# Chunked attention and a multiplicative FFN: half of the partition moves on ScalarE's queue, with another written-out order

## The chip, the cores and the metric

The kernel runs on one core of one Trainium2 chip. The metric is the time of one execution on the device in microseconds; lower is better. The kernel before took 247.61 us (median of 3 runs, 247.45 to 247.93).

A core has five engines that run their own instruction streams side by side: PE (TensorE, matrix products into PSUM), DVE (VectorE), ACT (ScalarE), POOL (GpSimd) and SP (SyncE). In this kernel POOL only issues loads and SP only issues moves and stores. Semaphores order the engines among each other. [...]

## The reference, cut to what matters

```python
batch, n_heads, seq, head_dim = (8, 8, 576, 64)          # q, k, v
chunk = 64; nc = S // chunk; scale = 1.0 / np.sqrt(D)
scores = scale * np.matmul(q_c, k_c.transpose(0, 1, 2, 4, 3))   # 64 x 64 in each chunk and head
attn = softmax(scores)                                   # exp, divided by the row's sum
out = np.matmul(attn, v_c)
x = out.transpose(0, 2, 1, 3).reshape(B * S, H * D)      # 4608 tokens x 512
a = x @ w1; b = x @ w2                                   # 512 -> 1024
return ((a * b) @ w3) @ w_out                            # 1024 -> 1024 -> 512
```

So 4608 tokens go through an attention within chunks of 64 tokens, and then through a feed-forward part. The kernel computes w3 @ w_out once (w3o) and so needs one product less for each token.

## The kernel before, in words

Tokens are handled in 18 pieces p of 256 (four chunks); two pieces make a group g = p // 2 of 512 tokens. Every step of the work has a letter and numbers, and the string ORDER (line 9) lists all steps in program order. The last loop of the kernel (line 412) walks through that string and emits the instructions of each step. All instructions are marked to stay in program order on their engine, so the string is the schedule: it sets the order on each engine's queue and, with it, the order of loads, moves and stores. There is no planner at run time.

The steps of attention for piece p are:

- q, k, v: loads from HBM, cast to bf16, on POOL's queue (`load`, L95). For the first piece q and k come through R (on SP and ACT) and are cast by K on ACT.
- T p.s (L188, DVE): transposes q (s=0) or k (s=1) in blocks of 32 x 32 into qkT.
- G g.a (`do_G`, L192, p of 8 and more): four moves between partitions each, qkT to qkm, 128 KB a move, so that the scores need half as many products. Pieces below 8 go without.
- S (PE): the scores, 64 small products; E (ACT): their exponential; P (PE): times v, with a column of ones for the row's sum; N p.u (DVE): reciprocal and product for half a piece, into xn.
- X p.u (DVE): transposes xn into xt (p below 8) or into xm, from which H g.a (`do_H`, L276) moves the blocks into xt by four moves of 64 KB each.

The steps of the feed-forward part are A p.j and B p.j (PE: x @ w1 and x @ w2 for a part j of the 1024 columns; one pair fills one PSUM buffer), C (ACT, L317: copies a out of PSUM), M (DVE, L332: times b, into ab), O (PE: with w3o, 256 tokens), Y (ACT: copies O's result), Q (SP: stores 512 KB). For p below 4, A and B take one piece and two values of j's columns at once; from p = 4 on they take a whole group, so p is then even. The weights are loaded by i (w1 and w2, a quarter at a time), h (w3, half at a time) and o (w_out); V, W and Z make w3o. D is a number of products with zeros into a buffer that is used next; it has no effect on the result.

Each engine waits for what it reads and for the release of the buffer that it writes. Those that matter are: PSUM with four buffers shared by S, P (two each), A/B, W and O, given out in program order, so that each waits for the one given out four before it; qk with 5, vbuf with 6, qkT, qkm, xm, e and o_sb with 2, a_sb, ab and xn with 3, w3T and xt with 4.

All moves and stores of before go through one function, on SP's queue:

```python
def move(dst, src):
    inorder(nc.sync.dma_start(dst, src))          # L180
```

Of the kernel before, what the change touches and what calls it, by code (L numbers as in the profile page):

```python
# [7 lines left out]

ORDER = """
R0 R1 v0 q1 k1 v1 i0 i2 i1 q2 k2 i3 v2 q3 k3 v3 q4 k4 h0 o h1 v4 D0.0.0.16.64 K0 T0.0 K1 T0.1 q5 k5  # L10
v5 D0.0.0.8.512 S0 T1.0 E0 T1.1 q6 k6 P0 v6 S1 N0.0 E1 N0.1 X0.0 X0.1 A0.0 B0.0 C0.0 P1 M0.0 A0.2
N1.0 B0.2 N1.1 A0.1 X1.0 X1.1 C0.1 B0.1 C0.2 A1.0 T2.0 B1.0 C1.0 A1.1 M0.1 M0.2 B1.1 C1.1 T2.1 q7 k7
v7 A0.3 M1.1 S2 C0.3 M1.0 B0.3 E2 M0.3 P2 A1.2 T3.0 B1.2 N2.0 A1.3 N2.1 B1.3 C1.3 X2.0 C1.2 X2.1
T3.1 q8 k8 v8 A2.0 M1.2 C2.0 S3 T4.0 B2.0 E3 A2.1 M1.3 B2.1 M2.0 C2.1 T4.1 q9 k9 P3 v9 A2.2 M2.1
B2.2 N3.0 A2.3 X3.0 N3.1 S4 C2.3 C2.2 X3.1 B2.3 E4 M2.2 A3.3 M2.3 B3.3 V0 A3.2 V1 B3.2 C3.2 V2 C3.3
A3.1 W0 V3 M3.3 M3.2 A3.0 V4 B3.1 C3.0 V5 Z0 B3.0 W1 C3.1 M3.1 T5.0 W2 V6 Z1 V7 T5.1 q10 k10 W3 Z2
M3.0 T6.0 T6.1 S5 Z3 P4 v10 q11 k11 E5 O0 N4.0 T7.0 T7.1 N4.1 O1 Y0 X4.0 Q0 T8.0 T8.1 P5 v11 q12 k12
Y1 X4.1 O2 N5.0 Q1 T9.0 N5.1 S6 T9.1 O3 E6 X5.0 G4.0 Y2 X5.1 G4.1 P6 v12 q13 k13 A4.0 Y3 N6.0 B4.0
X6.0 C4.0 Q2 A4.1 N6.1 B4.1 M4.0 C4.1 X6.1 S7 M4.1 A4.2 E7 T10.0 B4.2 C4.2 T10.1 P7 v13 q14 k14 A4.3
M4.2 N7.0 B4.3 C4.3 A4.4 M4.3 A4.5 N7.1 C4.4 B4.4 X7.0 C4.5 S8 M4.4 S9 E8 B4.5 T11.0 A4.6 E9 M4.5  # L20
B4.6 C4.6 X7.1 P8 v14 q15 k15 M4.6 A4.7 T11.1 B4.7 C4.7 N8.0 A6.0 G5.0 B6.0 M4.7 C6.0 N8.1 A6.1 M6.0
B6.1 G5.1 C6.1 X8.0 A6.4 M6.1 P9 v15 q16 k16 C6.4 B6.4 N9.0 A6.2 M6.4 B6.2 X8.1 C6.2 N9.1 A6.5 X9.0
B6.5 M6.2 H4.0 A6.3 X9.1 B6.3 C6.3 C6.5 A6.6 M6.3 H4.1 B6.6 M6.5 C6.6 T12.0 A6.7 S10 M6.6 S11 Q3 E10
B6.7 T12.1 O4 E11 T13.0 C6.7 M6.7 T13.1 P10 v16 q17 k17 Y4 A8.3 G6.0 N10.0 B8.3 N10.1 C8.3 A8.0 M8.3
G6.1 B8.0 T14.0 C8.0 P11 v17 A8.2 M8.0 X10.0 B8.2 C8.2 N11.0 O5 X10.1 N11.1 M8.2 X11.0 A8.1 X11.1
H5.0 Y5 T14.1 A8.5 C8.1 A8.4 T15.0 B8.5 H5.1 C8.4 C8.5 B8.1 A8.6 M8.1 B8.4 M8.5 C8.6 S12 M8.4 S13
E12 B8.6 T15.1 A8.7 E13 M8.6 G7.0 B8.7 C8.7 P12 M8.7 A10.3 N12.0 B10.3 Q4 C10.3 G7.1 A10.0 M10.3
A10.1 N12.1 C10.0 B10.0 C10.1 Q5 P13 M10.0 B10.1 N13.0 A10.6 M10.1 B10.6 C10.6 N13.1 A10.2 X12.0 S14
M10.6 C10.2 S15 B10.2 E14 T16.0 O6 E15 M10.2 T16.1 T17.0 A10.5 T17.1 Y6 P14 B10.5 C10.5 G8.0 O7
M10.5 N14.0 N14.1 Q6 G8.1 X12.1 X13.0 P15 Y7 A10.4 N15.0 B10.4 Q7 N15.1 C10.4 O8 X13.1 M10.4 X14.0  # L30
X14.1 S16 Y8 S17 A10.7 E16 Q8 B10.7 H6.0 C10.7 O9 E17 M10.7 X15.0 H6.1 O10 Y9 Q9 H7.0 P16 Y10 A12.2
N16.0 B12.2 X15.1 C12.2 O11 N16.1 H7.1 M12.2 Q10 P17 Y11 A12.7 N17.0 B12.7 X16.0 C12.7 A12.3 N17.1
A14.5 M12.7 C12.3 A12.0 B12.3 A12.4 M12.3 B12.4 X16.1 C12.4 X17.0 C12.0 A12.6 C14.5 M12.4 H8.0 B14.5
C12.6 B12.0 M14.5 B12.6 M12.0 Q11 A12.5 X17.1 M12.6 B12.5 H8.1 A14.7 A14.6 C14.7 C12.5 B14.6 C14.6
M12.5 B14.7 M14.6 A14.1 M14.7 A14.3 A16.1 C14.3 B14.1 C16.1 C14.1 B16.1 M14.1 B14.3 A16.3 M14.3
B16.3 C16.3 A12.1 M16.3 A14.0 M16.1 B12.1 C14.0 C12.1 A16.6 M12.1 A14.4 B14.0 C14.4 A16.5 M14.0
B14.4 C16.6 B16.6 O12 M16.6 B16.5 Y12 O13 C16.5 Q12 M16.5 M14.4 A14.2 Y13 A16.2 C14.2 Q13 B16.2
C16.2 B14.2 A16.7 M14.2 A16.4 C16.7 B16.4 B16.7 O14 M16.7 M16.2 A16.0 B16.0 C16.0 C16.4 O15 Y14
M16.4 M16.0 Q14 O16 Y15 Q15 Y16 Q16 O17
"""  # L40


# [1 line left out]
def kernel(  # L44
# [11 lines left out]
    nc = tc.nc  # L56
# [30 lines left out]
    def inorder(ins):  # L87
        tc.keep_in_program_order(ins)
        return ins
# [83 lines left out]
    blk = [slice(i * BL, (i + 1) * BL) for i in range(NB)]  # L173
    qkT_t, qkm_t, s_t, e_t, pv_t, xn_t, xm_t, xt_t = {}, {}, {}, {}, {}, {}, {}, {}
# [1 line left out]

    def move(dst, src):
        inorder(nc.sync.dma_start(dst, src))  # L180

    def do_T(p, s, h=None):

# [8 lines left out]
    def do_G(g, a):  # L192

        if a == 0:
            qkm_t[g] = asb.tile([P, 2, 2, 2, H, CH], bf, tag="qkm", bufs=2, name="qkm")

        for i in (0, 2, 1, 3):
            e = (i + a) % 2
            move(qkm_t[g][blk[i // 2 * 2 + e], i % 2], qkT_t[g][blk[i], e])

    def do_S(p, hh=None):
        g, m = divmod(p, 2)
# [50 lines left out]
    def new_xt(g):  # L253

        if g not in xt_t:
            xt_t[g] = asb.tile([P, KO * GT], bf, tag="xt", bufs=4, name="xt")
        return xt_t[g]
# [18 lines left out]
    def do_H(g, a):  # L276

        xt = new_xt(g)[:].rearrange("p (s c) -> p s c", s=2)
        for i in (0, 2, 1, 3):
            move(xt[blk[i // 2 * 2 + a], i % 2], xm_t[g][blk[i], a].rearrange("p o m t -> p (o m t)"))  # L280

    ab_t, ps_t, a_t, o_t = {}, {}, {}, {}

# [50 lines left out]
    def store(p, u0, u1, n0, n1, o_sb):  # L334
        move(out[p * PT + u0 * UT:p * PT + u1 * UT, n0:n1].rearrange("(u p) n -> p u n", p=UT), o_sb)
# [63 lines left out]
    def load_half3(i):  # L399
# [7 lines left out]


    do = {"q": load_q, "k": load_k, "v": load_v, "i": load_w12, "o": load_wo, "h": load_half3, "T": do_T, "S": do_S, "R": do_R, "K": do_K, "E": do_E, "G": do_G, "H": do_H,
          "P": do_P, "N": do_N, "X": do_X, "A": do_A, "B": do_B, "C": do_C, "M": do_M, "D": do_D, "V": do_V,  # L410
          "W": do_W, "Z": do_Z, "O": do_O, "Y": do_Y, "Q": do_Q}
# [32 lines left out]
```

The softmax here doesn't subtract the row's maximum and nothing guards it: scores larger than these inputs give would overflow.

## Time and profile before

| what | before |
|---|---|
| median of 3 runs | 247.61 us |
| the profiled execution | 247.45 us |
| its span | 245.3 us |
| PE busy | 228.4 us |
| DVE busy | 152.4 us |
| ACT busy | 83.3 us |
| POOL busy | 82.9 us |
| bytes in DMA packets | 37.63 MB |

The span runs from the first instruction to the last one of the profiled execution. What its time has beyond the span lies around it. Busy time is the sum of an engine's instructions; DMA-issuing instructions are not counted as busy on SP and ACT. The slices of the page divide the span into 40 equal parts of 6.13 us, and a digit is the busy share of a slice in tenths. In the lists of waits, each row names the waiting engine and line, then what released it, then the total in us, the number of times and the longest.

### The profile page before, as it was taken

The page shows a single profiled execution, that of the slowest core. Times are in us where ns is not written, and L with a number is a line of the kernel's source. Part 1 is how long each engine was busy: PE and PEld are TensorE (multiplying, and loading weights), DVE is VectorE, ACT ScalarE, POOL GpSimd, SP SyncE. Part 2 cuts the span into 40 slices and gives each one's busy share as a digit, 9 for nine tenths or more (in the row PEclk, how much of TensorE's full clock was granted, in tenths as well). Part 3 has the DMA queues.
Part 4 walks back from the last instruction along what each step waited for, and adds up shares of the span by engine and source line. Part 5 has one row for each costly group of instructions (what it writes and reads, how often), then busy time and mean ns, then how long its engine had stood idle before and what let it go on. Part 6 is the DMA issues. An engine that isn't in the chain of part 4 may idle for free.

```text
span 245.3 us, 6362 instructions
## 1 busy us (share of the span) xinstructions
PE 228.4 (93%) x2731; PEld 121.5 (50%) x2752; DVE 152.4 (62%) x232; ACT 83.3 (34%) x116; POOL 82.9 (34%) x110
## 2 busy tenths in 40 slices
PE   7268989999999989999899999999998999999994
PEld 3256878864545444444444444444443444444443
DVE  1847699978599488887887679672454534221110
ACT  2412423332422436225324524235333133142232
POOL 8845974576994148854440000000000000000000
PEclk9999999999999999999999999999999999999999
DMA  7999999999999999999999480554531500022044
GB/s 180 169 197 188 176 179 200 200 181 167 169 175 226 241 240 171 162 215 202 233 210 202 102 268 18 156 190 141 170 119 24 150 0 0 3 85 85 0 171 172
DMA packets 93595, 37.63 MB, mean 153 GB/s; under 512 B 75008, under 2 KB 86528, under 8 KB 93568
## 3 DMA queue, kind: packets, MB, share of 16 engines
q0 software_dynamic: 82592, 18.88, 83.5%
q1 hardware_dynamic: 9936, 17.83, 24.1%
q10 hardware_dynamic: 1040, 0.52, 0.8%
q8 instruction: 21, 0.34, 0.6%
q14 instruction: 6, 0.05, 0.1%
HBM read 38.80 MB, written 9.44 MB: 197 GB/s over the span
## 4 chain that ended last, share of the span: by engine, by line
PE 57%; DMA 25%; DVE 5%; POOL 5%; issue 3%; SPq 2%; ACT 1%; POOLq 0%; DVEq 0%
PE ab_ps L92 36%; PE o_ps L92 18%; DMA qk<-in_k_dram 10%; DMA qk<-in_q_dram 9%; DMA qkm<-qkT 3%; POOL vbuf L95 3%; DMA xt<-xm 3%; DVE qkT L188 2%; POOL qk L95 2%; SPq L180 2%; PE pv L92 2%; PE s_ps L92 1%; ACT a_sb L317 1%; DVE xn L251 1%; DVE ab L332 1%
## 5 line engine op out<-in xcount | busy, mean ns | idle before, releaser
L92 PE MATMUL ab_ps<-xt,w 128*128 128x512 bf16 (+1 forms) x697 | 132.0, 344 | 5.8 <-DVE xt L263 2.5
L92 PEld LDWEIGHTS <-w 128*128 128x128 bf16 x704 | 68.0, 99 | 59.8 <-issue 5.5
L332 DVE TENSOR_TENSOR ab<-a_sb,ab_ps 128x512 bf16<-128x512 f32 x72 | 47.9, 679 | 59.6 <-ACT a_sb L317 40.4
L317 ACT COPY a_sb<-ab_ps 128x512 f32<-128x512 f32 x72 | 41.2, 588 | 92.3 <-PE ab_ps L92 86.1
L92 PE MATMUL o_ps<-w3o,ab 128*128 128x512 bf16 (+1 forms) x284 | 63.9, 373 | 0.6
L188 DVE STREAM_TRANSPOSE qkT<-qk 128x1024 bf16<-128x1024 bf16 x36 | 45.8, 1296 | 5.9 <-ACT qk L139 5.3
L92 PEld LDWEIGHTS <-ab 128*128 128x128 bf16 x296 | 28.7, 98 | 32.9
L95 POOL DMA_DIRECT2D vbuf<-in_v_dram x40 | 34.0, 859 | 26.9 <-PE pv L92 8.6
L362 ACT COPY o_sb<-o_ps 128x1024 f32<-128x1024 f32 x17 | 17.2, 1013 | 40.5 <-PE o_ps L92 33.2
L251 DVE TENSOR_TENSOR xn<-pv,rc 128x512 bf16<-128x512 f32 x36 | 24.9, 692 | 1.2
L221 ACT ACTIVATE e<-s_ps 128x1024 bf16<-128x1024 f32 x17 | 17.0, 1026 | 9.2 <-PE s_ps L92 9.1
L95 POOL DMA_DIRECT2D qk<-in_q_dram x23 | 18.1, 791 | 5.3 <-DVE qkT L188 2.3
L95 POOL DMA_DIRECT2D qk<-in_k_dram x23 | 18.1, 794 | 4.7 <-DMA w<-in_moe_w_dram 2.4
L248 DVE RECIPROCAL rc<-pv 128x8 f32<-128x8 f32 x36 | 6.9, 192 | 13.4 <-PE pv L92 13.3
L92 PE MATMUL w_ps<-wo,w3T 128*128 128x512 bf16 x62 | 14.0, 379 | 0.1
L271 DVE STREAM_TRANSPOSE xm<-xn 128x512 bf16<-128x512 bf16 x20 | 13.6, 697 | 0.0
L95 POOL DMA_DIRECT2D w<-in_moe_w_dram x16 | 11.1, 697 | 6.4 <-DMA w<-in_moe_w_dram 3.9
L92 PEld LDWEIGHTS <-e 64*32 64x32 bf16 (+1 forms) x832 | 8.0, 98 | 7.9 <-issue 4.9
L92 PE MATMUL pv<-vbuf,e 64*32 64x65 bf16 (+1 forms) x832 | 10.2, 201 | 1.2 <-ACT e L221 1.1
L263 DVE STREAM_TRANSPOSE xt<-xn 128x512 bf16<-128x512 bf16 x16 | 10.7, 688 | 0.1
L373 DVE STREAM_TRANSPOSE w3T<-w 128x1024 bf16<-128x1024 bf16 x8 | 9.4, 1217 | 1.1 <-DVE ab L332 0.9
L92 PEld LDWEIGHTS <-w3T 128*128 128x128 bf16 x64 | 6.3, 98 | 7.1
(20 smaller groups left out, 38.2 us busy)
## 6 DMA issues: line engine op xcount, KB each, us to landing
out_dram<-o_sb SPq DMA_DIRECT2D x17, 512.0 KB, 3.0
qkm<-qkT SPq DMA_DIRECT2D x40, 128.0 KB, 6.2
vbuf<-in_v_dram POOLq DMA_DIRECT2D x32, 128.0 KB, 7.1
w<-in_moe_w_dram POOLq DMA_DIRECT2D x16, 256.0 KB, 9.2
qk<-in_q_dram POOLq DMA_DIRECT2D x11, 256.0 KB, 6.8
qk<-in_k_dram POOLq DMA_DIRECT2D x11, 256.0 KB, 8.0
xt<-xm SPq DMA_DIRECT2D x40, 64.0 KB, 2.3
wo<-in_moe_w_out_dram POOLq DMA_DIRECT2D x4, 256.0 KB, 9.3
```

The source lines that it names most:

```text
L92: return inorder(nc.tensor.matmul(*a, **kw))
L95: return inorder(nc.gpsimd.dma_start(dst, src))
L188: inorder(nc.vector.transpose(qkT_t[g][:, :, p % 2, s, heads(h)].rearrange("p e h (y t) -> p h t e y", t=2), qk_t[p][:, s, heads(h)].rearr ...
L221: inorder(nc.scalar.activation(e_t[p][:, :, heads(hh)], s_t[p][:].rearrange("p u (h q) -> p u h q", q=CH)[:, :, heads(hh)], Exp, scale=sca ...
L248: inorder(nc.vector.reciprocal(rc[:], pv[:, :, :, D:W]))
L251: inorder(nc.vector.tensor_mul(xn_t[p][:, u], pv[:, :, :, 0:D], rc.to_broadcast([P, 2, 4, D])))
L263: inorder(nc.vector.transpose(new_xt(g)[:].rearrange("p (o t) -> p o t", o=KO)[:, :, t0:t0 + UT] .rearrange("p o (m y) -> p m o y", y=BL), ...
L271: inorder(nc.vector.transpose(xm_t[g][:, u, :, m].rearrange("p o (c y) -> p c o y", y=BL), xn_t[p][:].rearrange("p u r m d -> p (u r) m d" ...
L317: inorder(nc.scalar.copy(a_t[p, j][:], ps_t[p, j][:, 0, :]))
L332: inorder(nc.vector.tensor_mul(o, view(a_t.pop((p, j))[:]), view(ps_t.pop((p, j))[:, 1, :])))
L362: inorder(nc.scalar.copy(o_sb[:], ps_t.pop(p)[:]))
L373: inorder(nc.vector.transpose(w3T_t[f][:].rearrange("p k (f y) -> p f k y", y=BL), w3[:, NB * f:NB * (f + 1), :].rearrange("p f (k x) -> p ...
```

## The change

Two things change.

First, `move` takes an engine. In `do_G` and `do_H` the four moves with a = 0 stay on SP's queue, and the four with a = 1 are issued by ACT, at their place in ACT's program order. There are ten such groups (G4.1 to G8.1, H4.1 to H8.1). Stores stay on SP.

Second, ORDER is another list of the same steps. The loads have i0 ahead of k1, v2 ahead of i3, v4 and o ahead of h0 and h1. D0.0.0.8.512 (eight products of 512 zeros before S0) goes, D0.1.0.4.512 (four, between P0 and S1) and D1.0.0.5.512 (five, between S1 and A0.0) come. A and B go through j in order 0 to 7 and each A is followed by its B; C and M follow in that order. W0 comes after all of piece 3 instead of before A3.0. O4, P11 and O5 stand ahead of the first A of p = 8, and then A/B of p = 8 and 10 run with only S and P between them; the O steps come in ones and pairs between groups. Q3 stands ahead of G5.

```diff
 ORDER = """
-R0 R1 v0 q1 k1 v1 i0 i2 i1 q2 k2 i3 v2 q3 k3 v3 q4 k4 h0 o h1 v4 D0.0.0.16.64 K0 T0.0 K1 T0.1 q5 k5
-v5 D0.0.0.8.512 S0 T1.0 E0 T1.1 q6 k6 P0 v6 S1 N0.0 E1 N0.1 X0.0 X0.1 A0.0 B0.0 C0.0 P1 M0.0 A0.2
-N1.0 B0.2 N1.1 A0.1 X1.0 X1.1 C0.1 B0.1 C0.2 A1.0 T2.0 B1.0 C1.0 A1.1 M0.1 M0.2 B1.1 C1.1 T2.1 q7 k7
 ...
-A3.1 W0 V3 M3.3 M3.2 A3.0 V4 B3.1 C3.0 V5 Z0 B3.0 W1 C3.1 M3.1 T5.0 W2 V6 Z1 V7 T5.1 q10 k10 W3 Z2
 ...
-B6.7 T12.1 O4 E11 T13.0 C6.7 M6.7 T13.1 P10 v16 q17 k17 Y4 A8.3 G6.0 N10.0 B8.3 N10.1 C8.3 A8.0 M8.3
-G6.1 B8.0 T14.0 C8.0 P11 v17 A8.2 M8.0 X10.0 B8.2 C8.2 N11.0 O5 X10.1 N11.1 M8.2 X11.0 A8.1 X11.1
 ...
+R0 R1 v0 q1 i0 k1 v1 i1 i2 q2 k2 v2 i3 q3 k3 v3 q4 k4 v4 o h0 h1 D0.0.0.16.64 K0 T0.0 K1 T0.1 q5 k5
+v5 S0 T1.0 E0 P0 D0.1.0.4.512 T1.1 q6 k6 v6 N0.0 S1 D1.0.0.5.512 X0.0 N0.1 X0.1 A0.0 E1 B0.0 C0.0 P1
+M0.0 A0.1 N1.0 X1.0 B0.1 C0.1 N1.1 A0.2 X1.1 B0.2 C0.2 M0.1 A1.0 T2.0 B1.0 C1.0 M0.2 A1.1 T2.1 q7 k7
+v7 B1.1 C1.1 M1.0 S2 M1.1 A0.3 E2 T3.0 B0.3 C0.3 P2 M0.3 A1.2 N2.0 X2.0 B1.2 C1.2 N2.1 A1.3 X2.1
+B1.3 C1.3 M1.2 A2.0 T3.1 q8 k8 v8 B2.0 C2.0 M1.3 S3 T4.0 A2.1 E3 M2.0 B2.1 T4.1 q9 k9 C2.1 P3 v9
+M2.1 A2.2 N3.0 B2.2 C2.2 X3.0 A2.3 N3.1 B2.3 X3.1 C2.3 M2.2 S4 M2.3 A3.0 E4 B3.0 C3.0 A3.1 M3.0 B3.1
+C3.1 V0 A3.2 M3.1 B3.2 C3.2 V1 A3.3 M3.2 B3.3 C3.3 V2 W0 M3.3 V3 W1 Z0 V4 V5 W2 Z1 V6 V7 T5.0 Z2 W3
+T5.1 q10 k10 T6.0 T6.1 P4 v10 q11 k11 Z3 S5 N4.0 O0 E5 X4.0 N4.1 X4.1 T7.0 O1 T7.1 Y0 Q0 T8.0 P5 v11
+q12 k12 Y1 S6 T8.1 O2 Q1 E6 N5.0 X5.0 N5.1 X5.1 O3 T9.0 T9.1 Y2 G4.0 P6 v12 q13 k13 A4.0 N6.0 B4.0
+G4.1 Y3 X6.0 N6.1 C4.0 A4.1 X6.1 B4.1 C4.1 M4.0 Q2 S7 Q3 M4.1 A4.2 E7 T10.0 B4.2 C4.2 T10.1 P7 v13
+q14 k14 A4.3 M4.2 B4.3 N7.0 C4.3 A4.4 X7.0 M4.3 B4.4 C4.4 N7.1 A4.5 M4.4 B4.5 C4.5 X7.1 S8 M4.5 S9
+E8 A4.6 T11.0 B4.6 E9 T11.1 P8 v14 q15 k15 C4.6 A4.7 M4.6 G5.0 B4.7 C4.7 N8.0 A6.0 M4.7 B6.0 N8.1
+C6.0 G5.1 A6.1 X8.0 B6.1 M6.0 C6.1 X8.1 P9 v15 q16 k16 A6.2 M6.1 N9.0 B6.2 C6.2 N9.1 A6.3 M6.2 B6.3
+C6.3 X9.0 A6.4 M6.3 B6.4 C6.4 X9.1 A6.5 T12.0 H4.0 B6.5 C6.5 M6.4 A6.6 M6.5 B6.6 T12.1 H4.1 C6.6 S10
+S11 M6.6 E10 A6.7 T13.0 B6.7 E11 P10 v16 q17 k17 T13.1 C6.7 O4 M6.7 G6.0 N10.0 N10.1 X10.0 G6.1 P11
+v17 Y4 X10.1 O5 N11.0 N11.1 Q4 X11.0 X11.1 T14.0 A8.0 H5.0 Y5 B8.0 T14.1 C8.0 A8.1 M8.0 B8.1 H5.1
+C8.1 T15.0 A8.2 B8.2 M8.1 C8.2 T15.1 Q5 A8.3 B8.3 C8.3 M8.2 G7.0 S12 M8.3 S13 E12 A8.4 T16.0 B8.4
+E13 G7.1 P12 T16.1 C8.4 A8.5 B8.5 M8.4 C8.5 N12.0 A8.6 M8.5 B8.6 C8.6 N12.1 A8.7 M8.6 B8.7 C8.7
+X12.0 P13 M8.7 A10.0 X12.1 B10.0 C10.0 N13.0 A10.1 M10.0 B10.1 N13.1 C10.1 A10.2 X13.0 B10.2 M10.1
+C10.2 X13.1 S14 S15 M10.2 E14 A10.3 H6.0 T17.0 B10.3 E15 P14 T17.1 C10.3 A10.4 H6.1 M10.3 B10.4
+C10.4 N14.0 A10.5 M10.4 B10.5 G8.0 C10.5 N14.1 A10.6 M10.5 B10.6 C10.6 X14.0 P15 G8.1 X14.1 A10.7
+M10.6 B10.7 N15.0 C10.7 O6 N15.1 M10.7 X15.0 X15.1 H7.0 S16 Y6 S17 O7 E16 E17 H7.1 P16 Y7 O8 Q6
 ...
 """
-    def move(dst, src):
-        inorder(nc.sync.dma_start(dst, src))
+    def move(dst, src, eng=None):
+        inorder((eng or nc.sync).dma_start(dst, src))
 ...
         for i in (0, 2, 1, 3):
             e = (i + a) % 2
-            move(qkm_t[g][blk[i // 2 * 2 + e], i % 2], qkT_t[g][blk[i], e])
+            move(qkm_t[g][blk[i // 2 * 2 + e], i % 2], qkT_t[g][blk[i], e], (nc.sync, nc.scalar)[a])
 ...
         for i in (0, 2, 1, 3):
-            move(xt[blk[i // 2 * 2 + a], i % 2], xm_t[g][blk[i], a].rearrange("p o m t -> p (o m t)"))
+            move(xt[blk[i // 2 * 2 + a], i % 2], xm_t[g][blk[i], a].rearrange("p o m t -> p (o m t)"),
+                 (nc.sync, nc.scalar)[a])
```

More of the change, by code (lines that the diff above doesn't have):

```diff
@@ L9 @@
 ORDER = """
-R0 R1 v0 q1 k1 v1 i0 i2 i1 q2 k2 i3 v2 q3 k3 v3 q4 k4 h0 o h1 v4 D0.0.0.16.64 K0 T0.0 K1 T0.1 q5 k5
-v5 D0.0.0.8.512 S0 T1.0 E0 T1.1 q6 k6 P0 v6 S1 N0.0 E1 N0.1 X0.0 X0.1 A0.0 B0.0 C0.0 P1 M0.0 A0.2
-N1.0 B0.2 N1.1 A0.1 X1.0 X1.1 C0.1 B0.1 C0.2 A1.0 T2.0 B1.0 C1.0 A1.1 M0.1 M0.2 B1.1 C1.1 T2.1 q7 k7
-v7 A0.3 M1.1 S2 C0.3 M1.0 B0.3 E2 M0.3 P2 A1.2 T3.0 B1.2 N2.0 A1.3 N2.1 B1.3 C1.3 X2.0 C1.2 X2.1
-T3.1 q8 k8 v8 A2.0 M1.2 C2.0 S3 T4.0 B2.0 E3 A2.1 M1.3 B2.1 M2.0 C2.1 T4.1 q9 k9 P3 v9 A2.2 M2.1
@@ L15 @@
-B2.2 N3.0 A2.3 X3.0 N3.1 S4 C2.3 C2.2 X3.1 B2.3 E4 M2.2 A3.3 M2.3 B3.3 V0 A3.2 V1 B3.2 C3.2 V2 C3.3
-A3.1 W0 V3 M3.3 M3.2 A3.0 V4 B3.1 C3.0 V5 Z0 B3.0 W1 C3.1 M3.1 T5.0 W2 V6 Z1 V7 T5.1 q10 k10 W3 Z2
-M3.0 T6.0 T6.1 S5 Z3 P4 v10 q11 k11 E5 O0 N4.0 T7.0 T7.1 N4.1 O1 Y0 X4.0 Q0 T8.0 T8.1 P5 v11 q12 k12
-Y1 X4.1 O2 N5.0 Q1 T9.0 N5.1 S6 T9.1 O3 E6 X5.0 G4.0 Y2 X5.1 G4.1 P6 v12 q13 k13 A4.0 Y3 N6.0 B4.0
-X6.0 C4.0 Q2 A4.1 N6.1 B4.1 M4.0 C4.1 X6.1 S7 M4.1 A4.2 E7 T10.0 B4.2 C4.2 T10.1 P7 v13 q14 k14 A4.3
@@ L20 @@
[L20 to L23, printed above, removed]
-B6.7 T12.1 O4 E11 T13.0 C6.7 M6.7 T13.1 P10 v16 q17 k17 Y4 A8.3 G6.0 N10.0 B8.3 N10.1 C8.3 A8.0 M8.3
@@ L25 @@
-G6.1 B8.0 T14.0 C8.0 P11 v17 A8.2 M8.0 X10.0 B8.2 C8.2 N11.0 O5 X10.1 N11.1 M8.2 X11.0 A8.1 X11.1
[L26 to L39, printed above, removed]
+R0 R1 v0 q1 i0 k1 v1 i1 i2 q2 k2 v2 i3 q3 k3 v3 q4 k4 v4 o h0 h1 D0.0.0.16.64 K0 T0.0 K1 T0.1 q5 k5
+v5 S0 T1.0 E0 P0 D0.1.0.4.512 T1.1 q6 k6 v6 N0.0 S1 D1.0.0.5.512 X0.0 N0.1 X0.1 A0.0 E1 B0.0 C0.0 P1
@@ new lines @@
+E13 G7.1 P12 T16.1 C8.4 A8.5 B8.5 M8.4 C8.5 N12.0 A8.6 M8.5 B8.6 C8.6 N12.1 A8.7 M8.6 B8.7 C8.7
[3 more added lines that the diff above has]
+M10.6 B10.7 N15.0 C10.7 O6 N15.1 M10.7 X15.0 X15.1 H7.0 S16 Y6 S17 O7 E16 E17 H7.1 P16 Y7 O8 Q6
+N16.0 Q7 N16.1 X16.0 X16.1 P17 Y8 A12.0 N17.0 Q8 B12.0 N17.1 C12.0 A12.1 X17.0 B12.1 M12.0 C12.1
@@ new lines @@
+X17.1 A12.2 M12.1 H8.0 B12.2 C12.2 A12.3 M12.2 B12.3 C12.3 H8.1 A12.4 M12.3 B12.4 C12.4 A12.5 M12.4
+B12.5 C12.5 A12.6 M12.5 B12.6 C12.6 A12.7 M12.6 B12.7 C12.7 O9 M12.7 O10 Y9 Q9 A14.0 Y10 B14.0 C14.0
+Q10 A14.1 M14.0 B14.1 C14.1 A14.2 M14.1 B14.2 C14.2 A14.3 M14.2 B14.3 C14.3 A14.4 M14.3 B14.4 C14.4
+A14.5 M14.4 B14.5 C14.5 A14.6 M14.5 B14.6 C14.6 A14.7 M14.6 B14.7 C14.7 O11 M14.7 O12 Y11 Q11 A16.0
+Y12 B16.0 C16.0 Q12 A16.1 M16.0 B16.1 C16.1 A16.2 M16.1 B16.2 C16.2 A16.3 M16.2 B16.3 C16.3 A16.4
@@ L40 @@
+M16.3 B16.4 C16.4 A16.5 M16.4 B16.5 C16.5 A16.6 M16.5 B16.6 C16.6 A16.7 M16.6 B16.7 C16.7 O13 M16.7
+O14 Y13 Q13 O15 Y14 Q14 O16 Y15 Q15 Y16 Q16 O17
 """
```

## The prediction

> **What bounds the kernel now.** I read the page's busy row first, then the waits of PE, then the stretches of ten microseconds, then the time line, and last the DMA issues.
>
> ```profile
> span 245.3 us, 6362 instructions
> PE 228.4 (93%) x2731; PEld 121.5 (50%) x2752; DVE 152.4 (62%) x232; ACT 83.3 (34%) x116; POOL 82.9 (34%) x110
> DVE  1847699978599488887887679672454534221110
> DMA  7999999999999999999999480554531500022044
> ```
>
> PE is busy 93% of the span. DVE looks idle at 62%, but its row of slices is at 7 to 9 for most of the first 160 us. The DMA engines are at 9 until slice 22, 135 us. So three resources are nearly full together, and a wait of any of them can surface as a PE gap.
>
> ```profile
> PE z_ps L92 <- DVE qkT L188: 3.8, 1, 3.8
> PE ab_ps L92 <- DVE xt L263: 2.5, 2, 1.9
> PE ab_ps L92 <- ACT a_sb L317: 1.8, 3, 0.8
> PE ab_ps L92 <- DMA xt<-xm: 0.8, 1, 0.8
> ```
>
> These are PE's waits (total, times, longest). Read with the time line: the first 9.4 us wait for q and k; the first A waits 1.9 at 13.4 for X0.1; later gaps are 0.67 at 22.8, 0.56 at 34.9, 0.72 at 87.4 ("issue"), 0.30 at 105.5, 0.16 at 115.3, 0.75 at 120.1 (A8.3 waits for H4's moves), 0.19 at 139.9 and 0.79 at 188.4 (PSUM held by late C copies). After 83.2, where A4.0 starts, they sum to 2.9.
>
> ```profile
> 15.27 3.57 PE L92 MATMUL ab_ps<-xt,w 128*128 128x256 bf16 x16 [1.90 <-DVE xt L263]
> 23.42 5.40 PE L92 MATMUL ab_ps<-xt,w 128*128 128x256 bf16 x48 [0.67 <-ACT a_sb L317]
> ```
>
> Start, duration: the same matmul takes 223 ns at 15 us and 112 ns at 23 us.
>
> ```profile
> 101.23 5.20 SPq L180 DMA_DIRECT2D qkm<-qkT  x8
> 109.89 4.94 SPq L180 DMA_DIRECT2D xt<-xm  x8
> ```
>
> A G or H pair of eight moves holds SP for about 5 us, 0.6 to 0.65 each.
>
> [...]
>
> **The change, part by part.** Prices are pitches of back-to-back rows: T 1.23, V 1.18, N (both instructions) 0.84, X 0.63, M 0.61 on DVE; C 0.48 (0.59 alone), E 0.92, Y 1.0 on ACT; on PE one A or one B 0.90 (p<4) or 0.86, S 0.63, P 0.63 (p<8) or 0.37, O and W 3.45. The steps of both orders sum to 221.4 us on PE, the same (dummies apart), so only gaps and the cold clock can differ. From A4.0 on, 158.8 us less 2.9 of gaps leaves 155.9.
>
> *Start.* Loads of i0 (two of 256 KB) now stand ahead of k1. In before k1 landed at 10.8 and w loads came about 1.35 apart, so k1 lands at about 13.5. T1.1, ahead of N0.0 on DVE, then ends at 14.9 and X0.1 at 17.8; before it was 15.1. The eight dummies before S0, hidden in the idle start, go. Four after P0 (0.43 cold, 1.7 us) lie in the wait for T1.1; five after S1 (2.1 us) end about 18.1, 0.3 past X0.1. A0.0 thus starts near 18.1, not 15.27, but PE has been fed since about 15, so A0.0 and B0.0 may be warm: 1.8 us instead of 3.57, less if the clock is still low. Ends of P1: 20.4 to 21.8 against 19.5, with 0.6 of cold matmuls still to come in before. What is late next? T3.0 waits for q3, which lands at 30.4 in both (the same loads precede it). Then M0.3, N2, X2 give 35.2 for X2.1, before 35.4, and A2.0 waits for it in both. So the late start is swallowed there. P3 ends at about 40.3 against 40.7. If k1 is a further 1.1 late the cover is gone and A2.0 is about 1.2 late.
>
> *The w3 stage.* wo and v4 now go ahead of h0: about 5.1 + 1.7 us, so h0's last part lands at 48.5 (41.8). V0 stands in DVE's queue behind M3.0, with M3.1 behind it. V0 ends at 49.8, M3.1 50.4, V1 51.6. W0 now follows all of p=3 and comes to its turn at 51.7: no stall, 1.8 us of cover for V0. A4.0 starts at 82.8 against 83.2: gain 0.4.
>
> *83 to 123 us.* Q3 moves ahead of G5: 0.5 MB at about 240 GB/s delays the loads by 2.1 us. k11 lands at 96.5 (94.4), so T11.1 ends near 98; M4.6 and N8.0 wait behind it, and their buffers are wanted at 99.5 and 101: covered. O4, P11 and O5 (7.3 us) now all precede A8.0, where before only O4 and P10 preceded A8.3. H4's last move is issued at about 112.5 and lands 6.2 later, 118.7; A8.0 comes at 123.3. The 0.75 gap goes. C and M follow j in order, so the gaps of 0.30, 0.19 and 0.79 from C held in ACT's line go too: 2.0 in all. I keep 0.72 of issue and 0.2 of small ones.
>
> *The moves on ACT.* Ten groups (G4.1 to G8.1, H4.1 to H8.1) of four are 40 issues by 0.6 to 0.65, 24 to 26 us, on an engine with 83 us of work in 245. Each group holds ACT 2.5 us, and the C, E and Y behind it, then their M on DVE, then PE through the four PSUM buffers. It also waits. The landing semaphores are eight, taken in turn by SP's and ACT's issues alike (the first two went to R0 on SP and R1 on ACT), so a move waits until the eighth issue before it has landed. Walk: G4.1 at 80, before Y3: no cost. G5.1 at 101.6–104.1: C6.1 is 2 us late, M6.1 ends 105.4, A6.3 wants its buffer at 105.7. H4.1 110.6–113.1, behind G5.1's landings (7.8 us after issue): C6.6 2 us late, covered by S10, S11 and A6.7. G6.1 at 116.9–119.5: under O4. H5.1 at 124.7: its fourth move waits for Q4's landing, 125 to 128, so C8.1 runs up to 3 us late, M8.1 ends 128.3 to 129.9, T15.1 follows, then M8.2 (130.1 to 131.7), for which A8.4 waits at 131.4. G7.1 stands between E13 and C8.4: C8.4 at 135.8, M8.4 at 136.5, A8.6 wants it at 135.3: 1.2. H6.1 and G8.1: C10.4 and C10.7 late inside about 1 us of slack. H7.1 is under O7, H8.1 inside four buffers. The stretch is narrow because DVE has 29.5 us of work (T14.0 to N15.1) beside 31.6 us of PE (A8.0 to O6). Below: no cost, if ACT's sequencer runs ahead. Above: 2.7 (0.3, 1.2 and another 1.2 of DVE lag not recovered). I take 1.1. SP loses the same issue time; the moves' hidden lead grows by 2.5 us per pair, worth nothing where the landing has cover.
>
> *Sum against the profiled execution* (247.45 us: span 245.3 and 2.15 around it): −0.4 by A4.0, −2.0 gaps gone, +1.1 ACT: −1.3, 246.15. The median of the three runs is 0.16 above the profiled one; I forecast 246.4. The tail is unchanged: from A12 on PE is dense in both orders.
>
> **Rivals.**
> 1. ACT runs ahead [...]: the 1.1 falls away, and if the clock is warm by A0.0 another 0.2: 245.2. For it: C usually sits waiting for PE (86 us of waits). Against: E12, E13 and C8.4 come back to back.
> 2. Slower: H5.1 and G7.1 hold C8.1 and C8.4 for landings in the tight stretch. If ACT is released at 131 rather than 128.5, M8.1 ends 132 and all of DVE's chain to T17.1 shifts 3 us with 1.7 us of slack; M8.4, M10.4 follow. With the like at G5.1/H4.1 (G5.1 landing at 114, as before, instead of 111.5: S10 waits 1.5), PE gains 4 to 5 us of gaps: 249.0. It decides when new gaps exceed 2.4 us. For it: DVE at 94% between T11.0 and N15.1, landings of 6 to 8 us until 130. Against: half of the issues are off SP, so each group starts 2.5 us sooner.
> 3. No change: the late k1 is not swallowed (+1.2) and cancels the removed gaps: 247.6.
>
> **Chances and range.** My forecast 0.45 (245.5 to 247.2), rival 1 0.13, rival 2 0.29, rival 3 0.13. Runs of this kernel spread 0.2% (247.45 to 247.93), about what can be told from no change: 247.1 to 248.1. Faster: 0.41 of the first and rival 1, 0.54; same: 0.04 and 0.11, 0.15; slower: the rest, 0.31. Leaving about 0.07 below and 0.12 above gives 244.9 to 249.8; the likeliest case alone spans 245.5 to 247.2.
>
> **What would show it.** Right: X0.1 ends near 17.8 yet A2.0 starts at 35 to 36; W0 starts without a gap near 51.7; A4.0 at 82 to 83.5; no gap ahead of A8.0; PE gaps between A8.3 and A8.7 of 0.3 to 1.5; ACT with 40 issues of 0.6. Wrong: A0.0 at 19 or later with cold matmuls beyond 21; DVE standing at V0 past 50 or at T11.1 past 99; C8.1 or C8.4 more than 3 us behind its A; S10 or S12 waiting for qkm. Most likely to upset it: landings on a shared semaphore that come later than I took, which hold ACT and not only SP.

## The result, and the profile after

The changed kernel takes 256.84 us (median of 4 runs, 256.5 to 257.84) where the kernel before, on the same chip, takes 247.77 us (4 runs as well). The ratio is 1.037, with a 95% interval of 1.034 to 1.041: 3.7% slower. The profiled execution took 257.84 us, the longest of the four. Of all executions in this document one, of the old order with moves on ACT (262.35 us), fell into a slower state, and its kernel's median leaves it out.

From the page of the changed kernel: the span, the busy times, and the slices of PE, of its granted clock and of DVE.

```profile
span 256.1 us, 6337 instructions
...
PE 232.0 (91%) x2731; PEld 122.3 (48%) x2753; DVE 153.5 (60%) x232; ACT 84.8 (33%) x116; POOL 82.7 (32%) x110
...
PE   1289999999999869999994899999999999999994
...
DVE  1565989798796657988992769874642143044000
...
PEclk9999999999999997999999599999999999999999
```

The span is 10.8 us longer, and PE's busy time has grown too, by 3.6 us, though its matrix products are the same but for the dummies. A slice is 6.4 us here. The row of PE dips twice, from 83 to 96 us and from 134 to 147 us, and the clock row dips behind each, from 96 and from 141 us on. Before, the clock was full from 20.5 us to the end of the work.

From the list of waits of the changed kernel (who waits, for what, total in us, times, longest):

```profile
ACT a_sb L318 <- DMA xt<-xm: 8.8, 2, 6.8
PE z_ps L92 <- DVE qkT L188: 7.9, 2, 7.2
...
DVE qkT L188 <- DMA vbuf<-in_v_dram: 3.8, 1, 3.8
...
PE ab_ps L92 <- DVE ab L333: 3.3, 2, 2.0
...
PE s_ps L92 <- DVE ab L333: 3.2, 1, 3.2
```

The second row is the start's. The others are new: ACT's copies (C) wait for moves between partitions, a transpose on DVE waits for a DMA, and PE waits for M (`ab`) because M holds PSUM. The chain of work that ended last names the causes. For the first dip it reads (start, duration):

```profile
83.34 9.13 DMA qkm<-qkT
...
92.74 2.48 DVE qkT L188 x2
95.22 0.56 DVE ab L333
95.78 0.04 issue
95.83 5.30 PE ab_ps L92 x16
```

A move has landed when its data has arrived and its semaphore says so. DVE stands for 3.84 us at T10.0, from the end of M4.1 at 88.9: the last of G4's moves lands at 92.5, and T10.0 starts at 92.74. M4.2 and M4.3 are behind T10.0 in DVE's queue, so PE gets its buffer for A4.4 only at 95.83. (The list of waits blames a load of v for this; DVE waits ahead of T10.0, from 89.37 to 92.70, on all eight semaphores on which the moves land, and the last to come was the moves'.) For the second dip the same chain reads:

```profile
123.31 4.63 DMA qkm<-qkT
...
128.00 10.13 DMA out_dram<-o_sb
138.13 0.02 issue
138.16 0.51 ACTq L180
...
138.77 0.59 ACT a_sb L318
139.36 0.02 issue
139.38 0.04 DVE ab L333
```

The store Q4 goes out at 128.00 and takes 10.1 us to land. Then, at 138.16, ACT can issue the last move of H5.1, and behind that move stands C8.1, whose A8.1 was ready at 132. The time line shows the price on PE:

```profile
129.43 7.07 PE L92 MATMUL ab_ps<-xt,w 128*128 128x512 bf16 x32
...
132.89 5.78 ACTq L180 DMA_DIRECT2D xt<-xm  x4
...
140.12 0.49 PE L92 MATMUL s_ps<-qkm 64*64 64x64 bf16 x32 [3.25 <-DVE ab L333]
...
141.90 3.57 PE L92 MATMUL ab_ps<-xt,w 128*128 128x512 bf16 x8 [1.28 <-DVE ab L333]
```

H5.1's four moves hold ACT's queue for 5.78 us (a hold, in what follows: the queue stands at a move that waits for an earlier landing), and PE has gaps of 3.25 and 1.28 us. The last row is the surprise: eight products in 3.57 us are 446 ns each, where the 32 of the first row took 221 ns each. (A row gives start, duration, what ran, the count, and in brackets the idle time before it and what ended it.) The granted clock is at half from 140.4 to 147.2, and likewise from 96.0 to 99.4 after the first gap.

### The profile page after: what moved, and what is told of

Same layout as the page of the kernel before. It is cut to its first block, busy times and chain, and to the rows that moved or that the text cites. A ratio compares the mean times of both kernels' runs of the same rounds, so it can differ in the third digit from the quotient of the medians.

```text
span 256.1 us, 6337 instructions
## 1 busy us (share of the span) xinstructions
PE 232.0 (91%) x2731; PEld 122.3 (48%) x2753; DVE 153.5 (60%) x232; ACT 84.8 (33%) x116; POOL 82.7 (32%) x110
## 4 chain that ended last, share of the span: by engine, by line
PE 70%; DMA 12%; DVE 9%; issue 2%; POOL 2%; ACT 1%; ACTq 1%; SPq 1%; DVEq 0%; POOLq 0%
PE ab_ps L92 40%; PE o_ps L92 19%; DMA qkm<-qkT 5%; PE w_ps L92 5%; DMA out_dram<-o_sb 4%; DVE qkT L188 4%; DMA qk<-in_k_dram 3%; PE z_ps L92 2%; PE s_ps L92 2%; DVE xn L251 2%; PE pv L92 2%; DVE xt L263 2%; DVE ab L333 2%; ACT a_sb L318 1%; ACTq L180 1%
## 5 line engine op out<-in xcount | busy, mean ns | idle before, releaser
L92 PEld LDWEIGHTS <-w 128*128 128x128 bf16 x704 | 68.8, 100 | 62.3 <-issue 9.5
L188 DVE STREAM_TRANSPOSE qkT<-qk 128x1024 bf16<-128x1024 bf16 x36 | 45.0, 1286 | 12.1 <-ACT qk L139 5.4
L95 POOL DMA_DIRECT2D qk<-in_k_dram x23 | 18.1, 791 | 5.7 <-DMA vbuf<-in_v_dram 2.3
L221 ACT ACTIVATE e<-s_ps 128x1024 bf16<-128x1024 f32 x16 | 15.9, 1032 | 2.2 <-PE s_ps L92 2.0
L263 DVE STREAM_TRANSPOSE xt<-xn 128x512 bf16<-128x512 bf16 x16 | 11.4, 711 | 0.5
L92 PEld LDWEIGHTS <-qkT 32*64 32x64 bf16 x512 | 5.5, 117 | 11.4 <-DVE qkT L188 9.4
## 6 DMA issues: line engine op xcount, KB each, us to landing
vbuf<-in_v_dram POOLq DMA_DIRECT2D x32, 128.0 KB, 7.8
qkm<-qkT SPq DMA_DIRECT2D x20, 128.0 KB, 5.9
qkm<-qkT ACTq DMA_DIRECT2D x20, 128.0 KB, 8.1
```

The costliest lines, as they stand in the source:

```text
L92: return inorder(nc.tensor.matmul(*a, **kw))
L95: return inorder(nc.gpsimd.dma_start(dst, src))
L188: inorder(nc.vector.transpose(qkT_t[g][:, :, p % 2, s, heads(h)].rearrange("p e h (y t) -> p h t e y", t=2), qk_t[p][:, s, heads(h)].rearr ...
L221: inorder(nc.scalar.activation(e_t[p][:, :, heads(hh)], s_t[p][:].rearrange("p u (h q) -> p u h q", q=CH)[:, :, heads(hh)], Exp, scale=sca ...
L263: inorder(nc.vector.transpose(new_xt(g)[:].rearrange("p (o t) -> p o t", o=KO)[:, :, t0:t0 + UT] .rearrange("p o (m y) -> p m o y", y=BL), ...
```

## The experiments

Times are medians; the ratio is to the kernel before on the same chip.

| kernel | us | ratio (95%) |
|---|---|---|
| changed kernel | 256.84 | 1.037 (1.034 to 1.041) |
| new order, all moves on SP | 245.48; again 245.08 | 0.992 (0.989 to 0.996); 0.993 (0.991 to 0.996) |
| old order, half of the moves on ACT | 256.09 | 1.036 (1.032 to 1.041) |
| changed, three qkT buffers | 253.89 | 1.027 (1.023 to 1.031) |
| changed, G4.1 on SP | 253.29 | 1.024 (1.021 to 1.026) |
| new order, all moves on SP, T10 put into g=4's buffer | 250.12 | 1.013 (1.011 to 1.016) |
| three qkT buffers, Q4 and Q5 later | 251.25 | 1.018 (1.012 to 1.024) |
| the same, and H5.1 on SP | 251.97 | 1.018 (1.015 to 1.021) |
| changed, G4.1, H5.1, G7.1 on SP | 245.50 | 0.993 (0.991 to 0.996) |
| new order with the old start, all on SP | 244.51; again 244.59 | 0.989 (0.987 to 0.992); 0.990 (0.988 to 0.993) |
| the same, seven groups on ACT | 244.95 | 0.992 (0.990 to 0.994) |

### The order alone

```diff
-            move(qkm_t[g][...], qkT_t[g][blk[i], e], (nc.sync, nc.scalar)[a])
+            move(qkm_t[g][...], qkT_t[g][blk[i], e])     # and so in do_H
```

> The changed order alone, with all moves between partitions on SyncE as before. Two waits (my theory: T10.0 is placed in the buffer that G4's moves still read, and C8.1 stands behind a move on ScalarE that waits for Q4's landing; both come from the moves on ScalarE): in this build qkT alternates between its two buffers, so T10.0 waits for PE alone; no gap over 1.2 us after 84 us, no half clock after 21 us, 246.0 to 247.8. Slow order (rival: the late k1 and the loads ahead of h0 do it): 252 or more with the gaps still there.

Measured: 245.48 us, and 245.08 in a later run. That is under the expected range, and faster than the kernel before by 0.7 to 0.8%. From the page of the second run:

```profile
PE   1279989999999999999999999999999999999994
...
PEclk9999999999999999999999999999999999999999
```

From 87.4 us to the end PE has no gap of 0.15 us or more, and the clock stays. The gaps of 0.15 us and more after A4.0, 2.9 us before, come to 0.28. The order isn't what made the kernel slow: it gains 1.4 to 1.9 us. The rival of a slow order falls.

### The moves alone

The opposite: ORDER of the kernel before, with `do_G` and `do_H` of the changed kernel.

> The order of the kernel before, with half of the moves on ScalarE. Two waits: here T10.0 is again placed in the buffer of g=4, so VectorE stands at T10.0 for 3 to 4 us until G4's moves land near 90, PE gets a gap of about 2 us and then half clock for 3 us or so: 3.5 to 5 us lost there; H5.1 stands behind other steps than in the new order and may or may not hold for a landing. 250.5 to 254. Slow order (rival): 248 to 249, as the moves cost little.

Measured: 256.09 us, 9.2 more than before, and above what I had expected. From its list of waits:

```profile
ACT a_sb L318 <- DMA xt<-xm: 8.3, 2, 5.6
...
ACT a_sb L318 <- DMA qkm<-qkT: 7.8, 2, 4.5
...
PE ab_ps L92 <- ACT a_sb L318: 5.4, 4, 2.9
ACT o_sb L363 <- DMA qkm<-qkT: 4.7, 1, 4.7
...
DVE qkT L188 <- DMA qkm<-qkT: 2.7, 1, 2.7
```

ACT's copies wait for moves here too, at more places, and T10.0 again waits for moves, now under their own name. PE's new gaps are 2.06, 1.08, 1.60, 2.51 and 2.87 us, but in this profiled execution the clock stays full over them. So the moves cost about 9 us in the old order and 11 in the new.

### T10's buffer

In the built program the qkT tile of g=5 lies, in the changed kernel, at the address of g=4's tile, which G4's moves are still reading; in the kernel before and in the new order alone it lies at that of g=3, which only S7 reads. The two tiles of a pool with two buffers were thus not used strictly in turn. With the moves alone on ACT the tile also lies at g=4's. The waits in the traces agree: T10.0 waits for eight landing semaphores in the changed kernel, for seven with the moves alone, and for none in the kernel before, in the new order alone and in the kernels below, except for the one that is made to use g=4's buffer. Three buffers take the wait away:

```diff
-            qkT_t[g] = asb.tile([P, 2, 2, 2, H, CH], bf, tag="qkT", bufs=2, name="qkT")
+            qkT_t[g] = asb.tile([P, 2, 2, 2, H, CH], bf, tag="qkT", bufs=3, name="qkT")
```

> The changed kernel with three qkT buffers instead of two, so that T10.0 needs no buffer that a move still reads. Two waits: the gap of 2.0 us near 94 and the half clock behind it vanish, about 5 us less from A4.0 to S8; the gaps near 137 to 142 stay, with the half clock after them: 251 to 253. Issue time (rival: 40 issues of 0.6 us on ScalarE make C and M late all along, and the waits only mark where it surfaces): 255 to 257.

Measured: 253.89 us, 0.9 over the expected range. The gap near 94 and the half clock behind it are gone, and PE's gaps of 4.35 and 1.14 us from 132.4 on stay. That the extra room isn't what helped is shown by putting one group of moves back on SP, after which the build places the tile at g=3's address again:

```diff
-            move(qkm_t[g][...], qkT_t[g][blk[i], e], (nc.sync, nc.scalar)[a])
+            move(qkm_t[g][...], qkT_t[g][blk[i], e], (nc.sync, nc.scalar)[a and g != 4])
```

> The changed kernel with G4.1 alone back on SyncE, two qkT buffers. Three holds (theory): T10.0 is again placed in the buffer of g=3, so that this equals the run with three buffers: no gap of 2.0 us near 94, no half clock there; the holds near 137 stay: 253 to 255. Rival (three buffers helped by their room, not by the choice of buffer): 256 to 258.

Measured: 253.29 us, as expected. The second stall is untouched, and the list of waits of this kernel names the store:

```profile
ACT a_sb L318 <- DMA out_dram<-o_sb: 8.2, 1, 8.2
...
PE s_ps L92 <- DVE ab L333: 4.7, 1, 4.7
```

The buffer by itself, without any move on ACT, was forced by naming the two buffers by hand:

```diff
+            tag="qkT%d" % (g % 2 if g < 5 else 1 - g % 2), bufs=1
```

> The changed order with all moves on SyncE, but qkT's two buffers are named by hand so that g=5 follows g=4 in the same one, as in the changed kernel. The buffer alone (theory): T10.0 waits until G4's last move has landed, near 92.7, though no move is on ScalarE: it starts 4 us later than with alternating buffers, a PE gap of 2.0 to 2.4 us ahead of A4.4; 2 to 2.5 us more than the new order's own time if the clock stays, 4 to 5 more if a stretch of half clock follows: 247.5 to 250. Rival (the moves on ScalarE are needed for the harm): within 0.5 us of the new order's own.

Measured: 250.12 us, 5.0 over the new order alone on the same chip and 0.1 over the expected range. From the time line of this kernel, and then of the new order alone (second run):

```profile
80.11 5.04 SPq L180 DMA_DIRECT2D qkm<-qkT  x8
...
92.63 2.46 DVE L189 STREAM_TRANSPOSE qkT<-qk 128x1024 bf16<-128x1024 bf16 x2 [4.79 <-DMA vbuf<-in_v_dram]
...
95.70 5.30 PE L92 MATMUL ab_ps<-xt,w 128*128 128x512 bf16 x16 [3.51 <-DVE ab L333]
```

```profile
87.86 2.49 DVE L188 STREAM_TRANSPOSE qkT<-qk 128x1024 bf16<-128x1024 bf16 x2
...
90.12 5.35 PE L92 MATMUL ab_ps<-xt,w 128*128 128x512 bf16 x23
```

All eight moves are on SP, and the stall is there: T10.0 at 92.63, after the last landing at 92.26, where the new order alone has it at 87.86. (The load of v named in the row isn't what held it: with the same loads, T10.0 of the new order alone doesn't wait.) PE loses 3.51 us, more than the 2.0 to 2.4 expected, and then runs 16 products in 5.30 us, 331 ns on average, with the clock at half for 3.4 us. In this stretch, then, the moves on ACT do harm through the choice of buffer, not through their issue.

### What holds ACT

The second stall seemed to come from the landing of the store Q4, so Q4 and Q5 were moved behind G7.1, with three qkT buffers:

```diff
-v17 Y4 X10.1 O5 N11.0 N11.1 Q4 X11.0 ...  T15.1 Q5 A8.3 ...  E13 G7.1 P12
+v17 Y4 X10.1 O5 N11.0 N11.1 X11.0 ...     T15.1 A8.3 ...     E13 G7.1 Q4 Q5 P12
```

> The changed kernel with three qkT buffers and with Q4 and Q5 moved behind G7.1, so that no move of H5.1 or G7.1 waits for the landing of a store. Two waits: no PE gap over 1.3 us after 84 us, no half clock after 21 us, 246 to 248.5. Issue time (rival): new gaps at other steps, 253 or more. Clock by itself (rival: PE falls to half clock whatever the gaps): the gaps vanish and the half clock stays, 250 to 252.

Measured: 251.25 us; the expected 246 to 248.5 was wrong. The time line of this kernel:

```profile
129.02 4.35 ACTq L180 DMA_DIRECT2D xt<-xm  x4
...
133.47 1.56 ACT L318 COPY a_sb<-ab_ps 128x512 f32<-128x512 f32 x3 [6.17 <-DMA qkm<-qkT]
...
134.83 0.45 PE L92 MATMUL s_ps<-qkm 64*64 64x64 bf16 x32 [1.19 <-DVE ab L333]
...
136.04 3.67 ACTq L180 DMA_DIRECT2D qkm<-qkT  x4
...
136.61 3.20 PE L92 MATMUL ab_ps<-xt,w 128*128 128x512 bf16 x8 [1.34 <-DVE ab L333]
```

H5.1 still holds ACT for 4.35 us, only now for the landings of G6, which were issued at 118.6 to 123.2 and came in from 125 to 133. Moves and stores of both queues share eight landing semaphores in turn (108, 109 and 112 to 117 in the traces; in the changed kernel Q4 lands on 116 at 138.13, and the last move of H5.1, the next on 116, goes at 138.16), and a pair of groups is eight moves: with the store out of the way, each move of H5 needs a move of G6 to have landed. So the thing to take away isn't the store but the group:

```diff
-                 (nc.sync, nc.scalar)[a])
+                 (nc.sync, nc.scalar)[a and g != 5])      # do_H
```

> As the run before it (three qkT buffers, Q4 and Q5 behind G7.1), but H5.1's four moves are issued by SyncE; the other nine groups stay on ScalarE. Landings hold ScalarE (my theory now: in the run before, H5.1 held ScalarE from 129.0 to 133.4 for the landings of G6, without any store): C8.1 runs at about 128, the gaps from 132 to 136.6 go; G7.1, next between E13 and C8.4, then waits on ScalarE for H5.1's landings, about 135 to 137, C8.4 is some 4 us later than with all moves on SyncE (133.4), and a gap of 1 to 3 us appears near A8.6: 247.5 to 250.5. Issue time alone (rival: 0.6 us each, whatever lands): H5.1's share is 2.4 us and 250 to 251 stays.

Measured: 251.97 us, not better, and 1.5 over the expected range. C8.1 runs at 128.3 as expected and the gaps near 132 to 136.6 are gone, but the loss came back whole at the next group. I had expected a gap of 1 to 3 us there. The time line of this kernel (the profiled execution took 253.63 us, the longest of five):

```profile
132.32 1.90 PE L92 MATMUL ab_ps<-xt,w 128*128 128x512 bf16 x8
...
135.60 5.19 ACTq L180 DMA_DIRECT2D qkm<-qkT  x4
...
140.89 1.07 ACT L318 COPY a_sb<-ab_ps 128x512 f32<-128x512 f32 x2 [6.77 <-DMA qkm<-qkT]
...
142.25 5.27 PE L92 MATMUL ab_ps<-xt,w 128*128 128x512 bf16 x16 [5.82 <-DVE ab L333]
```

ACT's queue stands from 132.6 to 135.6 for the landing of H5.0's last move, issues two moves, and stands again until 138.5 (H5.1's last landing) and 139.3. Only at 140.89 does C8.4 run, though A8.4 was done at about 133.3. Taken away one at a time, the holds move on. All three groups together:

```diff
-            move(..., (nc.sync, nc.scalar)[a])
+            move(..., (nc.sync, nc.scalar)[a and g not in (4, 7)])   # do_G
-                 (nc.sync, nc.scalar)[a])
+                 (nc.sync, nc.scalar)[a and g != 5])                 # do_H
```

> The changed kernel with two qkT buffers and Q4 where it was; only three of the ten groups, G4.1, H5.1 and G7.1, go back to SyncE, 28 issues stay on ScalarE. Three holds (theory): qkT alternates again, T10.0 needs no move to land, C8.1 and C8.4 stand behind no move: no PE gap over 1.3 us after 84 us, no half clock, 245 to 247. Issue time alone (rival): 70% of the loss stays, 253 or more.

Measured: 245.50 us, with two qkT buffers and Q4 in its old place. 28 of the 40 issues are still on ACT, and they show no cost against the new order alone (0.9934 with an interval of 0.991 to 0.996, against 0.9922 and 0.9933). In its time line the remaining groups look like this:

```profile
102.15 0.59 ACT L318 COPY a_sb<-ab_ps 128x512 f32<-128x512 f32 x1 [1.14 <-PE ab_ps L92]
102.21 2.54 ACTq L180 DMA_DIRECT2D qkm<-qkT  x4
...
104.85 0.59 ACT L318 COPY a_sb<-ab_ps 128x512 f32<-128x512 f32 x1 [2.11 <-DVE xm L271]
...
106.09 0.59 ACT L318 COPY a_sb<-ab_ps 128x512 f32<-128x512 f32 x1 [0.65 <-PE ab_ps L92]
```

A group without a hold takes 2.5 us, begins 0.06 us after the copy ahead of it began, and makes the next copy about 1 us late. The copies come 1.73 us apart and take 0.59, so the one after it is in time again. On SP, H5 and G7 still take 8.35 and 5.94 us for eight moves each in this kernel: the waiting is there as before, on a queue where nothing stands behind it but moves and stores.

### The start

```diff
-R0 R1 v0 q1 i0 k1 v1 i1 i2 q2 k2 v2 i3 ...  v5 S0 T1.0 E0 P0 D0.1.0.4.512 T1.1 ... S1 D1.0.0.5.512 X0.0
+R0 R1 v0 q1 k1 v1 i0 i2 i1 q2 k2 i3 v2 ...  v5 D0.0.0.8.512 S0 T1.0 E0 P0 T1.1 ... S1 X0.0
```

All moves are on SP here, so that only the start differs from the order alone.

> The changed order with all moves on SyncE, and its start as before: k1 ahead of i0, the eight dummies before S0, none after P0 and S1. Start swallowed (the prediction's step: A2.0 waits for q3's landing in any case): A0.0 at 15 to 15.5, but A2.0 within 0.4 us of 36.0, and the time within 0.3 us of the new order's own, 245.2 to 245.9. Start not swallowed (rival: the late k1 is what makes A2.0 0.9 us later than in the kernel before): A2.0 at 35.5 or earlier, 244.2 to 244.9.

> The changed order with all moves on SyncE once more, beside the same with the start of before, on one chip. Start not swallowed (rival): 0.7 to 1.2 us above the one with the old start. Start swallowed (the prediction's step): within 0.4 us of it.

> The changed order with the start of before, all moves on SyncE, once more. Start not swallowed (rival): 0.7 to 1.2 us below the run beside it. Start swallowed: within 0.4 us of it.

Measured: 244.51 us at first. That is what the rival had expected, with A2.0 at 35.5, against 36.35 in the first run of the order alone, which ran on another chip. Side by side it is 244.59 with the old start against 245.08 with the new one. The intervals (0.988 to 0.993 and 0.991 to 0.996) overlap, and the difference of 0.5 lies between the two expectations. In these profiles A2.0 starts at 35.6 in both, and A4.0 at 82.9 and 83.0. That speaks for a start that is swallowed at least in most part; whether it costs the half microsecond stays open.

> The changed order with the start of before, and seven of the ten groups of moves on ScalarE (G4.1, H5.1 and G7.1 on SyncE). Landings, not issue, cost (theory): 28 issues of 0.6 us on ScalarE change nothing, within 0.4 us of the same kernel with all moves on SyncE. Issue time (rival): 1 us or more above it.

Measured: 244.95 us, 0.36 above the same kernel with all moves on SP, with overlapping intervals. Again no cost of 28 issues is seen; a few tenths would not be. The best kernel here is the changed order with all moves on SP, with the old or the new start: 1% under the kernel before, and nothing is gained by putting any move on ACT.

### Where the microseconds went

Starts of steps on PE (of their first weight load) in the profiled executions:

| | A4.0 | S10 | A8.0 | A10.0 | O17 |
|---|---|---|---|---|---|
| new order alone (second run) | 83.0 | 112.7 | 122.7 | 139.0 | 235.5 |
| with T10 in g=4's buffer | 82.9 | 118.2 | 128.2 | 144.4 | 241.0 |
| changed, G4.1 on SP | 83.1 | 113.3 | 124.0 | 147.8 | 244.3 |
| changed | 83.9 | 118.6 | 129.2 | 152.4 | 248.9 |

From A4.0 to S10 the order alone takes 29.7 us, and 35.3 and 34.7 where T10 is in g=4's buffer. From A8.0 to A10.0 it takes 16.3, and 23.8 and 23.2 where H5.1 and G7.1 are on ACT. Outside these two stretches there is 0.9 before A4.0 and 0.6 from S10 to A8.0. So the 13.4 us between the first and the last row are 5.0 of the buffer, 6.9 of the held ACT, and 1.5 of the rest.

In the first stretch gaps account for 2.9 us more than in the order alone (2.00, and 1.14 against 0.28), and half clock for 3.4 us, at 446 against 221 ns a product, is worth half of that, 1.7. In the second, gaps are 4.5 us, and 5.5 busy us at half clock are worth 2.8. Each pair adds up to its 5.0 and 6.9 within half a microsecond.

The first and last rows are extremes: the changed kernel's profiled execution is the longest of its four, that of the order alone (244.36 us) the shortest of its seven. By the ratios of the medians the moves cost about 11 us, 7.4 of it for H5.1 and G7.1 (1.0235 against 0.9934) and 3.4, give or take 1.1, for the buffer (1.0374 against 1.0235). The buffer's 3.4 is less than its 5.0 above. The mean granted clock is 0.980 in the profiled execution and 0.986 to 0.987 in the three others, which is one stretch of 3.41 us at half clock fewer, worth 1.7 us. It may be the one behind the first gap, which was only 2.00 us long; the traces at hand don't show it.

## Why the prediction was wrong

**The start** held in the main: A0.0 at 17.6 (I had 18.1), and A2.0 at 36.6, 0.6 past the range; but with the same loads A2.0 came at 35.6 in the second run of the order alone, so the lateness isn't shown to be the order's. **The w3 stage** held as far as the gap goes: W0 follows without one, at 52.7. A4.0 at 82.8 was forecast: the order alone has 83.7 and 83.0 in its two runs, the changed kernel 83.9, the kernel before 83.2, so that the gain of 0.4 isn't shown. **83 to 123 us** held for the order: no gap ahead of A8.0, the gaps from C gone. Its two terms, −0.4 and −2.0, sum to −2.4; the order alone measured −1.4 to −1.9.

**The moves on ACT** is the step that failed. It came to 1.1 us, bounded at 2.7, and measured about 11. Three statements in it were wrong.

- "G4.1 at 80, before Y3: no cost." I followed what stands behind a move on ACT and not who waits for its data to be read: T10.0, which writes a qkT buffer. The sum took it for granted that this was g=3's. It was g=4's, and T10.0 stood until 92.7. This alone is 5.0 us in the new order, and 3.4 of the changed kernel's time by the medians.
- "its fourth move waits for Q4's landing, 125 to 128." The wait was named rightly, and it ended at 138.1. Q4 was issued at 128.0, because Y4 stood on ACT behind G6.1, which itself took until 126.8; and the landing took 10.1 us. Even in the order alone, where nothing is late, Q4 goes out at 123.6 and lands at 131.5, 3.5 later than forecast, and SP is through with H5 at 132.0. In the kernel before, the four stores issued until 117 us had taken 6.5 to 8.0 us to land, which the figure of 128 passes over. The chain of a hold behind a hold was not followed through. C8.1 was 7 us behind A8.1, not up to 3.
- G7.1 at 1.2: with H5.1 out of the way it costs PE 5.8 us by itself, since it waits for H5's landings.

**The clock** was priced for the start only. That A0.0 and B0.0 "may be warm" was an estimate, and it did not hold: in the changed kernel their products took 208 ns in the mean from 18.01 on, as against 223 before, and the clock was full from 20.9 (before, from 20.5). Later the changed kernel has 3.41 us of half clock after a gap of 2.00, and 6.83 us after one of 3.25. The prediction's gaps of up to 5 us in rival 2 might have met the same; its 249.0 has no such term.

**Rival 2** had the mechanism: H5.1 and G7.1 hold C8.1 and C8.4 for landings. Its size was off. It released ACT at 131, it was 138.8; it saw neither the buffer nor the clock. Its further wait, S10 for the moves of G5, did not come. **Rival 1** had nearly the number that the issues would have cost by themselves, nothing (245.2, against 245.5 with seven groups), but not for its reason: that ACT runs ahead, so that an issue hides behind a copy that is still waiting, was my assumption, with no row of before to show it. In the lines of that kernel an issue begins 0.06 us after the copy ahead of it has started, and the copy had waited 1.14 us for PE: the issue overlaps the copy's run, not its wait. What absorbs the rest is the slack between copies. **Rival 3** fell: the late k1 cost about half a microsecond or nothing side by side, not 1.2, and the order gained all the same.

**The sum** has a slip: 246.15 and 0.16 are 246.31, where 246.4 was forecast. It changes nothing in the outcome.

What I had called most likely to upset the forecast, landings on a shared semaphore that hold ACT, did so in the second dip. The first dip held DVE, not ACT.

## What to carry to other kernels

The issue of a DMA was cheap on ACT where it had slack (28 issues showed no cost), but it carries its waits with it. So follow for every issue which earlier landing it waits for, when that one was itself issued, and who stands behind on the queue; SP took 8.35 us over H5 in the kernel with three groups on SP and PE had no gap there, where 5.78 us on ACT stopped PE. Look up in the built program which tile shares an address with which, since a transfer that is issued from elsewhere can change that for a step that the edit doesn't touch; and count for PE's gaps the half clock that can follow them (3.41 us of it after a gap of 2.00 in the changed kernel).

## What the runs showed of the hardware

- Half clock came behind 2 us and more of idle time on PE, but not each time. In the changed kernel it lasted 3.41 us from 96.01 and 6.83 us, twice as long, from 140.38, and these starts are 44.37 us apart, 13 of the shorter stretch: the clock changes on a grid of 3.41 us here. Over all profiled kernels that have such records (two have none), from 84 to 200 us, every window of this grid at full clock with 2.00 us of idle time or more (2.00, 2.13, 2.38, 2.53, 2.59, 3.16, 3.18) was followed by half clock, and none with 1.99 or less (1.99, 1.76, 1.47, 1.40, ...) was. Where between these the edge lies isn't sharp, since the ends of products are modelled in the profile. The old order with the moves on ACT had gaps of 2.51 and 2.87 us, each split over two windows, and kept its clock: the 28 products from 136.06 on, behind the first of them, took 6.21 us, 222 ns each.
- Which engine issues four moves changed the address that the build gave to a later tile of another step. Why it did so wasn't found out.
- A 512 KB store lands after 2.9 us in the median of the changed kernel, but took 10.1 us when issued at 128.0. That one isn't alone: the four stores issued before 90 us took 6.7 to 9.3 us, and Q4 took 7.9 us in the order alone. All of these went out while loads were still coming: the last packet of a load ends at 138.45 in the changed kernel, and the order alone issues its last loads from 124.4 on, after its Q4 at 123.6. What slowed them wasn't tried.
